# Weight folding of a linear-attention and softplus kernel: first weight block loaded ahead of batch 0's queries, each block folded right behind its turning, bias rows among the folds

## The chip, the cores and the metric

The kernel runs on one core of one Trainium2 chip. The metric is the device time of one execution in microseconds (us), taken over several runs; the changed kernel and the kernel before are timed in turn on the same chip. Times are quoted as medians with their range. A ratio is the mean time of one kernel's runs in the fast state over that of the other's in the same rounds, so it is not quite the ratio of the medians. The span of a profile (first to last instruction) is some 1.8 us shorter than the time of the same run.

## The reference, cut to what matters

```python
B, H, S, D = 8, 8, 576, 64
q_p = concat(relu(q) * cos_w, relu(q) * sin_w)        # the same for k_p
kv  = einsum('bhsf,bhsd->bhfd', k_p, v);  z = sum_s k_p
x   = einsum('bhsf,bhfd->bhsd', q_p, kv) / (einsum('bhsf,bhf->bhs', q_p, z) + 1e-6)
h   = x.reshape(4608, 512) @ w_in                     # w_in 512 x 2048
out = softplus(h) @ w_out                             # w_out 2048 x 512
```

The kernel uses that the hidden values are small: softplus(h) is close to ln 2 + h/2, so `softplus(x @ w_in) @ w_out` becomes `x @ W_c + b` with `W_c = 0.5 * w_in @ w_out` and `b = ln 2` times the column sums of `w_out`. It checks at the end that this is accurate enough, with an exact path behind an `if` that is not taken here. The product `w_in @ w_out` ("folding") is done once, at the start, in 8 blocks of 256 hidden columns.

## The kernel before

All loads are issued by GpSimd in one order and are cast from f32 to bf16 on the way (the page of this kernel has 36.70 MB read from HBM for 18.35 MB landed by the load queue). Batch 0's keys and values come first, then its queries, then the weight blocks, then the other batches.

```python
for part in range(2):
    load(0, "q", part)                        # two halves of batch 0's queries
for j in range(BLOCKS):                       # 8 weight blocks
    cols = slice(128 * FB * j, 128 * FB * (j + 1))
    nc.gpsimd.dma_start(w_in_sb[:, :, cols], w_in_r[:, :, cols])
    ...
    nc.gpsimd.dma_start(w_out_rows(FB * j, FB), w_out_r[:, FB * j : FB * (j + 1), :])
... # then batches 1, 2
```

PE's program for the first stage: 18 idle matmuls on constant data ("spin"), batch 0's values (`key_values`), then batch 0's four tiles of 128 tokens and the weights side by side. `turn_w_in(j)` transposes one weight block on PE and DVE copies it out of PSUM; `fold(j - 1)` multiplies the block turned one step earlier, so that no fold waits for DVE's copy (in the profile none of the 64 fold matmuls has a wait; two turns have, 0.19 and 0.82 us for DVE's copies):

```python
for hq in range(2):
    ...
    key_values(0, hq)
    spin(5 - 2 * hq)                          # idle matmuls, no work of the result
mark_eps()
for hq in range(2):
    relu_q(0, hq, nc.vector)
mark_perm()
turn_queries(0, split=True)
turn_queries(1, big_ps, split=True)
for j in range(BLOCKS + 1):
    if j < BLOCKS:
        turn_w_in(j)
    if j == 0:
        turn_queries(2, big_ps)
        attend(0, qt_ps)
        ...
    if j > 0:
        fold(j - 1, wc_ps)
    if 0 < j < 4:
        attend(j, qt_ps)
    if 0 < j < 5:
        turn_x(j - 1)
    ...
```

Behind it come W_c's scaling, ten matmuls for the bias, and batch 1. From there the kernel goes tile by tile (36 in all): `turn_queries` (two tiles ahead), `attend`, `turn_x`, `emit` (the product with W_c), while GpSimd applies relu to a later batch's keys and queries.

## Time and profile before

| | kernel before |
|---|---|
| median of the runs beside the changed kernel | 136.25 us (135.75 to 138.92, 6 runs) |
| span of the profile | 135.1 us |
| PE, ACT, DVE busy | 86%, 74%, 73% |
| end of the folds, of the bias (chain) | 40.28, 42.86 us |
| first query turn of batch 1, of batch 2 | 46.76, 55.90 us |

The reader is to see the 5 in the clock row, in the fifth slice: for some 3.4 us PE ran at about half clock (the 6 and the 5 at the end lie behind the last matmul). The view of busy time by stretch makes it plain (columns: from:to, length, then busy time of PE, PEld, DVE, ACT and POOL, granted clock, share of the DMA engines, GB/s):

```profile
10.20:13.60 3.40, 1.14 (x39) 0.86 (x39) 2.20 (x9) 2.24 (x9) 1.94 (x3) 1.00 1.24 199
13.60:17.00 3.40, 3.25 (x18) 1.67 (x17) 2.22 (x5) 1.18 (x3) 1.56 (x3) 0.50 1.36 201
```

PE was busy for only 1.14 of 3.40 us while it waited for batch 0's second half, and in the 3.40 us after that its clock was 0.50.

### The profile page before, as it was taken

How to read it: one execution, taken by the hardware profiler on the slowest of the kernel's cores; microseconds unless marked ns; L12 is line 12 of the kernel's file. 1: busy time of each engine (PE TensorE's matmuls, PEld its weight loads, DVE VectorE, ACT ScalarE, POOL GpSimd, SP SyncE). 2: the span in 40 equal slices, each digit the busy share in tenths (PEclk: the TensorE clock that was granted, in tenths of full speed). 3: DMA queues.
4: the chain of work that ended last, by engine and by line, in shares of the span. 5: the costliest groups of instructions: out<-in, count | busy, mean ns of one | idle time of the engine just before them, and what ended most of it. 6: DMA issues, size and time to landing. Idle time of an engine off the chain costs nothing.

```text
span 135.1 us, 4531 instructions
## 1 busy us (share of the span) xinstructions
PE 116.6 (86%) x1888; PEld 75.3 (56%) x1888; DVE 98.9 (73%) x198; ACT 100.6 (74%) x183; POOL 66.0 (49%) x84
## 2 busy tenths in 40 slices
PE   5993979999799987998989998999999999998700
PEld 2342466665344665675657676667577676764200
DVE  1356694567892589999987998898996995867710
ACT  3596345778989474989977996997988997998300
POOL 6995446454544118989889759063406610000000
PEclk9999599999999999999999999999999999999965
DMA  1999999999999999999999999999997397983450
GB/s 12 177 170 199 200 203 199 200 202 202 207 208 207 207 208 209 206 210 206 209 208 207 216 264 251 266 239 272 238 253 236 131 325 276 355 296 124 160 167 10
DMA packets 24683, 28.15 MB, mean 208 GB/s; under 512 B 1616, under 2 KB 20048, under 8 KB 24656
## 3 DMA queue, kind: packets, MB, share of 16 engines
q0 software_dynamic: 19152, 18.35, 83.0%
q1 hardware_dynamic: 5424, 9.31, 19.8%
q8 instruction: 17, 0.28, 0.8%
q10 hardware_dynamic: 80, 0.13, 0.3%
q14 instruction: 10, 0.08, 0.2%
HBM read 36.70 MB, written 9.44 MB: 341 GB/s over the span
## 4 chain that ended last, share of the span: by engine, by line
PE 44%; DVE 20%; ACT 14%; DMA 9%; issue 6%; POOL 2%; ACTq 0%; POOLq 0%
PE o_ps L404 10%; PE q_ps L321 8%; ACT qT L333 7%; PE wc_ps L233 6%; DVE vcs L280 6%; DMA v_sb<-in_v_dram 6%; PE kv_ps L294 5%; PE num_ps L351 4%; DVE o_sb L426 4%; DMA passed<-rden 3%; DVE x L362 3%; ACT xT_all L375 3%; ACT x L380 3%; PE xT_ps L371 3%; DVE w_inT L216 2%
## 5 line engine op out<-in xcount | busy, mean ns | idle before, releaser
L333 ACT CAST qT<-q_ps 128x1024 bf16<-128x1024 f32 x33 | 33.4, 1014 | 9.8 <-PE q_ps L321 9.8
L404 PE MATMUL o_ps<-W_c,xT_all 128*128 128x512 bf16 x128 | 32.8, 379 | 0.6 <-DVE o_sb L426 0.6
L280 DVE TENSOR_TENSOR vcs<-v_sb,cs_wide 128x1152 bf16<-128x1152 bf16 x32 | 28.5, 905 | 1.6 <-DMA v_sb<-in_v_dram 1.6
L426 DVE TENSOR_TENSOR o_sb<-o_ps,b_bc 128x512 f32<-128x512 f32 x32 | 22.0, 687 | 6.7 <-PE o_ps L404 6.5
L362 DVE TENSOR_TENSOR x<-num_ps,rden 128x512 bf16<-128x512 f32 x36 | 24.9, 691 | 2.4 <-DVE rden L358 0.5
L375 ACT CAST xT_all<-xT_ps 128x512 bf16<-128x512 f32 x36 | 21.4, 595 | 4.4 <-PE xT_ps L371 4.4
L321 PE MATMUL q_ps<-diag,q_r 128*128 128x256 bf16 x144 | 22.6, 282 | 1.9 <-ACT qT L333 0.9
L256 POOL TENSOR_SCALAR k_sb<-k_sb 128x1152 bf16<-128x1152 bf16 x12 | 14.2, 1196 | 16.7 <-DMA k_sb<-in_k_dram 16.7
L263 POOL TENSOR_SCALAR q_r<-q_sb 128x1152 bf16<-128x1152 bf16 x13 | 16.2, 1267 | 8.2 <-DMA q_sb<-in_q_dram 8.1
L380 ACT ACTIVATE x<-x,zero_b 128x1024 bf16<-128x1024 bf16 x17 | 19.7, 1158 | 0.0
L404 PEld LDWEIGHTS <-xT_all 128*128 128x128 bf16 x144 | 12.8, 98 | 10.6 <-issue 1.0
L321 PEld LDWEIGHTS <-q_r 128*128 128x128 bf16 x144 | 12.0, 99 | 6.8 <-issue 1.3
L351 PE MATMUL num_ps<-kvblk,qT 64*128 64x65 bf16 (+1 forms) x640 | 15.7, 193 | 0.0
L233 PE MATMUL wc_ps<-w_out_sb,w_inT 128*128 128x512 bf16 x64 | 15.0, 379 | 0.0
L294 PE MATMUL kv_ps<-vcs,k_sb 64*64 64x132 bf16 x576 | 11.3, 219 | 2.9 <-DVE eps L174 2.3
L371 PE MATMUL xT_ps<-perm,x 128*128 128x128 bf16 x128 | 12.4, 219 | 0.6 <-ACT xT_all L375 0.6
L341 PEld LDWEIGHTS <-warm 128*128 128x128 bf16 x72 | 6.9, 98 | 9.3 <-issue 1.7
L371 PEld LDWEIGHTS <-x 128*128 128x128 bf16 x144 | 10.6, 98 | 2.2 <-issue 0.6
L224 ACT ACTIVATE w_square<-w_inT,zero_b 128x512 bf16<-128x512 bf16 x16 | 11.6, 723 | 0.3
L351 PEld LDWEIGHTS <-qT 64*128 64x128 bf16 (+1 forms) x640 | 11.2, 97 | 0.8
L294 PEld LDWEIGHTS <-k_sb 64*64 64x64 bf16 x576 | 9.0, 106 | 4.7 <-issue 3.0
L358 DVE RECIPROCAL rden<-num_ps 128x8 f32<-128x8 f32 x36 | 7.1, 197 | 5.4 <-PE num_ps L351 5.4
(72 smaller groups left out, 132.0 us busy)
## 6 DMA issues: line engine op xcount, KB each, us to landing
out_dram<-o_sb SPq DMA_DIRECT2D x32, 256.0 KB
k_sb<-in_k_dram POOLq DMA_DIRECT2D x7, 576.0 KB, 14.8
v_sb<-in_v_dram POOLq DMA_DIRECT2D x6, 576.0 KB, 12.5
q_sb<-in_q_dram POOLq DMA_DIRECT2D x6, 576.0 KB, 18.0
xT_all<-in_moe_w_in_dram POOLq DMA_DIRECT2D x8, 256.0 KB, 10.6
w_out_sb<-in_moe_w_out_dram POOLq DMA_DIRECT2D x8, 256.0 KB, 10.6
v_sb<-in_v_dram POOLq DMA_DIRECT2D x4, 288.0 KB, 9.0
q_sb<-in_q_dram POOLq DMA_DIRECT2D x4, 288.0 KB, 9.9
```

The source lines that it names most:

```text
L233: nc.tensor.matmul(ps[g // 2][:, g % 2, :], w_inT_rows(ft)[:, g * 128 : (g + 1) * 128], w_out_rows(ft)[:, 0], start=(ft == 0), stop=(ft == ...
L280: nc.vector.tensor_mul(view(vcs, [T * 2 * VW, 2], [2 * VW, T], [1, D], offset=2 * hq * T * 2 * VW + c * VW), kqv[b, "v"][:, 2 * hq : 2 * h ...
L294: nc.tensor.matmul(kv[64 * i : 64 * i + 64, h2, :, :VW], k_r[rows, 2 * hq + i, t, :], vcs[rows, 2 * hq + i, t, :, :], start=(t == 0), stop ...
L321: nc.tensor.matmul(ps[:, j // 2, 256 * (j % 2) : 256 * (j % 2) + 256], q_rs[b][:, hq, t, :, :], diag[:, t, :, :], start=True, stop=True, s ...
L333: nc.scalar.copy(view(qT, [512, 2], [64, 2], [128, 4], [1, 64]), view(ps, [1, 1024]))
L351: nc.tensor.matmul(num[p0 : p0 + m, i, C * g : C * g + C], qTs[n][rows, hq, 2 * c + h2, p0 : p0 + m], blk_bufs[b % 3][rows, hq, h2, c, :], ...
L362: nc.vector.tensor_mul(xs[n // 2][:, n % 2], view(num, [C, 4], [512, 2], [1, D]), view(rden, [1, 4], [4, 2], [0, D]),)
L371: nc.tensor.matmul(ps[:, g, :], x[:, g, :, :], perm if len(tiles[n]) == 1 else ident, start=True, stop=True, skip_group_check=True,)
L375: nc.scalar.copy(xT_all[:, n], ps)
L380: nc.scalar.activation(x, x, ACT.Square, bias=zero_b, accum_out=x_norm[:, n : n + 1])
L404: nc.tensor.matmul(ps, xT_all[:, n, g, :], W_c[:, g, :], start=(g == 0), stop=(g == 3))
L426: nc.vector.tensor_add(o_sb, ps, b_bc)
```

## The change

The intent: PE has little to do between batch 0's values and its queries, so the first weight block is loaded there, turned and folded. From then on each block is folded right behind its own turning, with a query turn, an attend or an x turn between the turning and the fold to cover DVE's copy. Part of the bias rows moves among the folds and four output tiles move ahead of batch 1's values.

```diff
-    for part in range(2):
-        load(0, "q", part)
     for j in range(BLOCKS):
+        if j == 1:
+            for part in range(2):
+                load(0, "q", part)
...
+    turn_w_in(0)
     mark_eps()
+    fold(0, wc_ps)
     for hq in range(2):
         relu_q(0, hq, nc.vector)
     mark_perm()
     turn_queries(0, split=True)
-    turn_queries(1, big_ps, split=True)
...
+    attend(0, qt_ps)
+    beside = {
+        1: [lambda: turn_queries(1, split=True)],
+        2: [lambda: attend(1, qt_ps), lambda: turn_x(0)],
+        3: [lambda: turn_queries(2, split=True), lambda: turn_x(1)],
+        4: [lambda: attend(2, qt_ps)],
+        5: [lambda: turn_queries(3, split=True), lambda: turn_x(2)],
+        6: [lambda: attend(3, qt_ps)],
+        7: [lambda: turn_x(3), lambda: bias(range(8, 12))],
+    }
+    for j in range(1, BLOCKS):
+        turn_w_in(j)
+        for work_j in beside[j]:
+            work_j()
+        fold(j, wc_ps)
...
+    bias(range(12, FO))
...
-    early = [emit(0, xt_bank()), emit(1)]
-    for hq in range(2):
-        key_values(1, hq)
+    early = [emit(0, xt_bank()), emit(1)]         # finish both, then
+    early = [emit(2, xt_bank()), emit(3)]
+    for hq in range(2):
+        key_values(1, hq)
     turn_queries(4, split=True)
```

(The sums of `w_out`'s rows on DVE are also spread over four blocks, and query turns use one PSUM buffer in place of two.)

More of the change, by code (lines that the diff above doesn't have):

```diff
@@ L236, in fold, with sum_w_out, bias @@
             )
-    def sum_w_out(quarter):
-        rows = w_out_rows(4 * quarter, 4)
-        nc.vector.tensor_add(w_tmp if quarter else w_sum, rows[:, :2, :], rows[:, 2:, :])
-        if quarter:
+    def sum_w_out(step):
+        if step < 2:
+            rows = w_out_rows(4 * step, 4)
+            nc.vector.tensor_add(w_tmp if step else w_sum, rows[:, :2, :], rows[:, 2:, :])
+        elif step == 2:
             nc.vector.tensor_add(w_sum, w_sum, w_tmp)
+        else:
             nc.vector.tensor_add(w_tmp[:, 0, :], w_sum[:, 0, :], w_sum[:, 1, :])
-    def bias():
-        ps = o_ps.tile([128, D_MODEL], F32, tag="o", name="b_ps")
-        nc.tensor.matmul(ps, ones, w_tmp[:, 0, :], start=True, stop=False)
-        for ft in range(8, FO):
-            nc.tensor.matmul(ps, ones_b, w_out_rows(ft)[:, 0], start=False, stop=(ft == FO - 1))
-        nc.scalar.mul(b_bc, ps, LN2)
+    bias_ps = []
+    def bias(rows):
+        if not bias_ps:
+            bias_ps.append(qt_ps.tile([128, D_MODEL], F32, tag="qt", name="b_ps"))
+        for ft in rows:
+            nc.tensor.matmul(bias_ps[0], ones_b, w_out_rows(ft)[:, 0], start=(ft == 8), stop=False)
+        if rows.stop == FO:
+            nc.tensor.matmul(bias_ps[0], ones, w_tmp[:, 0, :], start=False, stop=True)
+            nc.scalar.mul(b_bc, bias_ps[0], LN2)
     def relu_k(b, engine, hps=slice(0, 4)):
@@ L451 @@
         spin(5 - 2 * hq)
+    xt_bank = lambda: xt_ps.tile([128, D_MODEL], F32, tag="xt", name="o_xt")
+    big_bank = lambda: big_ps.tile([128, 2, D_MODEL], F32, tag="big", name="o_big")[:, 0]
+    wc_ps = [big_ps.tile([128, 2, D_MODEL], F32, tag="big", name=f"wc_ps{r}") for r in range(2)]
+    turn_w_in(0)
     mark_eps()
+    fold(0, wc_ps)
     for hq in range(2):
@@ L456 @@
     turn_queries(0, split=True)
-    turn_queries(1, big_ps, split=True)
-    xt_bank = lambda: xt_ps.tile([128, D_MODEL], F32, tag="xt", name="o_xt")
-    big_bank = lambda: big_ps.tile([128, 2, D_MODEL], F32, tag="big", name="o_big")[:, 0]
-    for j in range(BLOCKS + 1):
-        if j < BLOCKS:
-            turn_w_in(j)
-        if j == 0:
-            turn_queries(2, big_ps)
-            attend(0, qt_ps)
-            nc.vector.tensor_copy(ident_f, ident)
-        if j == 1:
-            turn_queries(3)
-            wc_ps = [
-                big_ps.tile([128, 2, D_MODEL], F32, tag="big", name=f"wc_ps{r}") for r in range(2)
-            ]
-        if j > 0:
-            fold(j - 1, wc_ps)
-        if 0 < j < 4:
-            attend(j, qt_ps)
-        if 0 < j < 5:
-            turn_x(j - 1)
+    attend(0, qt_ps)
+    nc.vector.tensor_copy(ident_f, ident)
+    beside = {
[12 more added lines that the diff above has]
+        fold(j, wc_ps)
+        for ft in range(FB * (j - 1), FB * j):
+            square_w(ft)
+        if j in (3, 5, 6, 7):
+            sum_w_out((3, 5, 6, 7).index(j))
         if j == 6:
             square_x(0)
-        if 0 < j < 8:
-            for ft in range(FB * (j - 1), FB * j):
-                square_w(ft)
-        if j in (3, 5):
-            sum_w_out((j - 3) // 2)
-        if j == 6:
             mark_values(1)
@@ L489 @@
         nc.scalar.mul(W_c[:, g, :], wc_ps[g // 2][:, g % 2, :], 0.5)
+    bias(range(12, FO))
     for ft in range(7 * FB, FO):
         square_w(ft)
-    bias()
     square_x(1)
@@ L496 @@
             scale_values(1, hq, c)
+    early = [emit(0, xt_bank()), emit(1)]
+    for done in early:
+        finish(*done)
     relu_k(1, nc.vector)
     relu_q(1, 0, nc.gpsimd)
-    early = [emit(0, xt_bank()), emit(1)]
+    early = [emit(2, xt_bank()), emit(3)]
+    finish(*early[0])
+    relu_q(1, 1, nc.vector)
     for hq in range(2):
         key_values(1, hq)
-    for done in early:
-        finish(*done)
-    relu_q(1, 1, nc.vector)
-    early = [emit(2, xt_bank())]
     turn_queries(4, split=True)
-    early.append(emit(3))
+    finish(*early[1])
     turn_queries(5, big_ps)
-    for done in early:
-        finish(*done)
     pool_relu(2)
```

## The prediction

> **What bounds the kernel now.** I read the page first: PE is busy 86% of the span of 135.1 us, ACT 74%, DVE 73%, and the DMA row of the slices is at 9 from the second slice to slice 31, about 105 us. So two things run through the kernel side by side: PE's stream, in program order, and the stream of loads on the GpSimd queue. The chain of waits says which of them sets the end around the changed stage (columns: start us, length us, what):
>
> ```profile
> 36.22 0.61 PE wT_ps L210 x8
> 36.83 3.45 PE wc_ps L233 x16
> 40.28 0.86 PE b_ps L248 x2
> 41.14 1.73 PE b_ps L250 x8
> 42.86 0.86 PE o_xt L404 x4
> 43.73 0.89 PE o_ps L404 x4
> 44.62 1.18 PE kv_ps L294 x63
> 45.79 0.97 PE o_xt L404 x4
> 46.76 0.45 PE q_ps L321 x4
> ```
>
> The reader is to see the end of the weight stage: the last two blocks are folded together (16 matmuls, to 40.28), the bias follows (10 matmuls, to 42.86), then two output tiles, the values of batch 1, a third output tile, and only at 46.76 the first query turn of batch 1 (tile 4). The change shortens exactly this piece.
>
> The second view is the timeline of GpSimd, because batch 2 is prepared there:
>
> ```profile
> 43.03 1.14 POOL L263 TENSOR_SCALAR q_r<-q_sb 128x1152 bf16<-128x1152 bf16 x1 [0.26 <-DMA q_sb<-in_q_dram]
> ...
> 50.12 2.26 POOL L256 TENSOR_SCALAR k_sb<-k_sb 128x1152 bf16<-128x1152 bf16 x2 [5.81 <-DMA k_sb<-in_k_dram]
> 52.97 2.81 POOL L263 TENSOR_SCALAR q_r<-q_sb 128x1152 bf16<-128x1152 bf16 x2 [0.59 <-DMA q_sb<-in_q_dram]
> 55.72 0.79 POOL L75 DMA_DIRECT2D v_sb<-in_v_dram  x1
> ```
>
> GpSimd sits idle 5.81 us until the keys of batch 2 land at 50.1, and again until its queries land at 52.97; their relu is done at about 55.75. The third view, PE's timeline, shows what waits for that:
>
> ```profile
> 54.76 0.19 PE L341 MATMUL num_ps<-eps_b,warm 128*128 128x4 bf16 x2
> 54.88 0.43 PE L351 MATMUL num_ps<-kvblk,qT 64*128 64x65 bf16 x16
> 55.25 0.72 PE L294 MATMUL kv_ps<-vcs,k_sb 64*64 64x132 bf16 x36
> 55.90 0.61 PE L321 MATMUL q_ps<-diag,q_r 128*128 128x256 bf16 x4
> ```
>
> By program order (tiles 0-3 are batch 0, 4-7 batch 1, 8 is the rest of both, 9 the first of batch 2; queries are turned two tiles ahead) the turn at 55.90 is tile 9's, the first that reads batch 2's relu'd queries. PE came to it at 55.90, the queries were ready at about 55.75. **The slack is 0.15 us.** PE arrives here just in time; it cannot pass this point earlier unless the queries come earlier.
>
> Do they? They are the 30th of the loads, and the windows view gives the same 201 to 208 GB/s landed in 10-36, 36-53 and 53-72 us. There is no gap in the stream to close.
>
> [...]The page of this kernel has 36.70 MB read for 18.35 MB landed by the load queue (f32 cast to bf16), so 201 to 208 GB/s landed is some 400 to 415 read (my doubling)[...]. [...]the issue of each load waits for the eighth before it, in order. [...]the second query relu of batch 2 took 1.70 us beside a DVE scaling of values (54.02-54.77), the median of that row is 1.15.[...]
>
> **The change part by part.**
> 1. The load order. Only w_in block 0, w_out block 0 and the two query halves of batch 0 change places. From the issues that wait for them, w_in block 0 landed at 15.5, w_out block 0 at 16.8, the query halves at 12.8 and 14.2. After: the weights some 2.7 us earlier (12.8, 14.1), the queries 2.6 us later (15.4, 16.8). From block 1 on (18.2) all landings stay: same bytes, same order, same wait for the eighth before. Block 7 lands at about 34.8 (w_in) and 36.0 (w_out); batch 1's keys at 41.5, its query halves at 43.0 and, one half load later, about 44.4; batch 2's keys at 50.1 and queries at 53.0.
> 2. The folds. One block (8 matmuls) is 1.73 us, a turn of weights 0.45, a query turn 0.54, an attend 0.54, a turn of x 0.22 to 0.33, half the bias rows 4 x 0.216 = 0.86. In PE's stream from the first weight turn to the end of the last fold: 8 x 1.73 + 8 x 0.45 + 4 x 0.54 + 4 x 0.54 + 4 x 0.28 + 0.86 = 23.7 us. From 12.9 that is 36.6 at best; the last block lands at 36.0, so not before 36.1 + 1.73 = 37.9. A fold now stands right behind its own turning, and must wait for DVE's two copies (0.75 us) less what PE does between; I choose 0.15 us of idle a block beyond the DMA's floor, 8 x 0.15 = 1.2, so the folds end at about **39** instead of 40.28. The range of this is 38 to 40.5.
> 3. The bias. It was 0.86 + 1.73 = 2.59 us after the folds; now 0.86 of it lies among them, 1.73 remains: PE is free at about 40.8 instead of 42.86, **2.1 us earlier**.
> 4. DVE and ACT. Two query evacuations of 1.01 us on ACT become 0.59 on ACT with 0.69 on DVE: ACT loses 0.84, DVE gains 1.38. The four sums of w_out are the same work, spread over four blocks. ACT had 0.50 us of idle before W_c, so this keeps W_c from being late.
> 5. Behind the weights, four output tiles (4 x 0.88) now stand before batch 1's values. They fill PE from 40.8 to about 44.3, the values take 1.2, so PE is at tile 4's turn at about 45.5; its queries are ready at 44.4 + 0.74 (DVE relu) = 45.2. So tile 4 is turned at about 45.5 instead of 46.76: of 2.1 us, **1.3 us** are left.
> 6. The next five tiles keep this lead, until tile 9's turn. There PE arrives at 55.90 - 1.3 = 54.6, the queries are ready at 52.97 + 2 x 1.15 = 55.3 (no collision with DVE) to 55.75 (as before). So the turn starts at 55.3 to 55.75, and **0.15 to 0.6 us** of the lead are left; I take 0.4. The rest turns into a wait of PE of about 0.9 us.
>
> Behind this PE's stream is the same, with a mean of some 2.3 us a tile. Later load limits do not bind: batch 3's queries are ready at 64.33 for a turn at 65.98, batch 7's at 108.6 for a turn at 110.48, so 0.4 us fit into both. The sum is 136.33 - 0.4 = **135.9 us**.
>
> **Rivals.** (a) The whole 1.3 to 2.1 us arrive at the end: 134.2 to 135.0. For it: the chain runs on PE here. Against it: 0.15 us of slack at tile 9, and a load stream with no gap. It needs batch 2's queries over a microsecond earlier, and no part of the change does that. (b) The new order makes the weight stage slower: fold waits for DVE's copy, DVE has 1.38 us more, one PSUM buffer serves query turns, attends and the bias in turn, and PE cannot hide it. Then tile 4 comes later than 46.76, and each such microsecond is fully paid, as there is no slack: 137 to 138. Against it: 1.5 us of room between 39 and the old end. (c) DVE and GpSimd collide more in 53 to 56 us, as DVE's scalings move earlier: both query relus at 1.7 us put the turn at 56.4, some 0.5 us later: 136.8. (d) PE's unexplained 0.85 us of issue at 70.36 falls elsewhere or goes: up to 0.85 either way.
>
> **Range and chances.** The cap gives 135.7 to 136.2; (c), (d) and the spread between runs widen it to **135.0 to 136.9**. Faster by over 2% is below 133.6, which needs 2.7 us, more than the change saves even on PE: 0.03. Slower by over 2% is above 139.1, and needs (b) in full: 0.03. Within 2%: 0.94.
>
> **What would show it.** Right: folds end near 39, tile 4's turn near 45.5, batch 2's queries still land near 53, a new wait of PE of 0.5 to 1.3 us on GpSimd's relu (L270 in the changed kernel) before tile 9's turn, which starts at 55.3 to 55.8. Wrong: tile 9's turn well before 55, as the loads came earlier; tile 4's turn after 46.8, so rival (b); or a lead at 56 us that is lost or grows later, which would mean that a limit behind tile 9 matters that I took as settled.

The sum came to 136.33 - 0.4 = 135.9 us. What the trace shows is 201 to 208 GB/s landed from 10 to 72 us. The order of the loads is in GpSimd's timeline: of the 11th to the 33rd load, 22 were issued when the eighth before had landed (those at 12.83 and 14.21 us had waited 0.73 and 0.62 us for the query halves), and the one at 35.09 waited for DVE's sum. That a relu takes longer beside a scaling, which rival (c) builds on, was read from the one overlap given, 1.70 us against a median of 1.15.

## More of the kernel before

The two rows are PE's busy share and the granted TensorE clock, both in tenths, over 40 slices of 3.38 us:

```profile
PE   5993979999799987998989998999999999998700
...
PEclk9999599999999999999999999999999999999965
```

## The result, and the profile after

The changed kernel took 141.19 us in the median (139.76 to 142.88, 6 runs) against 136.25: the ratio of the fast runs is 1.029, 95% interval 1.025 to 1.033. It is slower, and lies outside my range. Its runs split: three at 142.0 to 142.9, which are marked slow, and three at 139.8 to 140.4. The first profile belongs to a slow run, so I use it only to see what to look for. Its rows of PE's busy share and granted clock:

```profile
PE   5944758999999985999979899799999999998700
...
PEclk9999996899999999599999999999999999999996
```

The clock falls twice, at 22 us and at 56 us. In PE's timeline of this run (columns: start us, length us, instruction, then what PE waited for):

```profile
20.00 0.19 PE L348 MATMUL num_ps<-eps_b,warm 128*128 128x4 bf16 x2 [1.40 <-DVE qT L336]
...
21.58 0.61 PE L328 MATMUL q_ps<-diag,q_r 128*128 128x256 bf16 x4 [0.48 <-DVE x L369]
22.05 3.43 PE L234 MATMUL wc_ps<-w_out_sb,w_inT 128*128 128x512 bf16 x8
...
26.64 1.89 PE L234 MATMUL wc_ps<-w_out_sb,w_inT 128*128 128x512 bf16 x8
```

the fold of block 1 takes 3.43 us, that of block 2, the same eight matmuls, 1.89. And in busy time by stretch, each of the two falls follows 3.4 us in which PE was busy about half the time (1.72 and 1.87 us of 3.40), with a clock of 0.51 and 0.50 after it:

```profile
18.80:22.20 3.40, 1.72 (x31) 1.28 (x31) 2.27 (x6) 0.42 (x1) 1.78 (x3) 1.00 1.36 200
22.20:25.60 3.40, 3.40 (x12) 1.39 (x11) 0.82 (x2) 2.11 (x5) 1.92 (x3) 0.51 1.34 202
53.00:56.40 3.40, 1.87 (x31) 1.32 (x31) 2.44 (x7) 2.10 (x3) 3.10 (x3) 1.00 1.20 208
56.40:59.80 3.40, 3.40 (x38) 2.06 (x39) 2.05 (x5) 2.64 (x4) 2.85 (x5) 0.50 1.22 207
```

Summed over such a stretch, one minus the clock gives 1.71 us of PE time lost at full clock. So I formed these theories. **Clock**: the change leaves PE waiting in a place where this makes the granted clock fall, and the slowdown is these stretches. Rivals: **query chain** (batch 0's queries, 2.6 us later, hold up PE in program order at full clock), **fold behind turning** (waits for DVE's copies and for the one PSUM buffer), and **collision** (being late makes DVE and GpSimd meet more often). The prediction's own **cap** (batch 2's queries hold tile 9) was to be tested too.

### The profile page after: what moved, and what is told of

Its sections match the earlier page's. It is cut to its first block, busy times and chain, and to the rows that moved or that the text cites. A ratio compares the mean times of both kernels' runs of the same rounds, so it can differ in the third digit from the quotient of the medians.

```text
span 141.1 us, 4527 instructions
## 1 busy us (share of the span) xinstructions
PE 118.6 (84%) x1888; PEld 75.8 (54%) x1888; DVE 102.3 (72%) x200; ACT 99.4 (70%) x183; POOL 68.0 (48%) x84
## 4 chain that ended last, share of the span: by engine, by line
PE 42%; DVE 26%; ACT 10%; DMA 9%; issue 7%; POOL 2%; DVEq 0%; ACTq 0%; POOLq 0%
DVE vcs L287 10%; PE o_ps L411 10%; PE wc_ps L234 7%; PE q_ps L328 7%; DMA v_sb<-in_v_dram 6%; ACT qT L340 6%; DVE o_sb L433 6%; PE kv_ps L301 4%; DVE x L369 4%; DMA passed<-rden 3%; PE num_ps L358 3%; PE xT_ps L378 2%; PE wT_ps L211 2%; ACT qT L336 2%; ACT x L387 1%
## 5 line engine op out<-in xcount | busy, mean ns | idle before, releaser
L340 ACT CAST qT<-q_ps 128x1024 bf16<-128x1024 f32 x31 | 31.5, 1015 | 7.0 <-PE q_ps L328 7.0
L411 PE MATMUL o_ps<-W_c,xT_all 128*128 128x512 bf16 x128 | 33.7, 387 | 1.4 <-DVE o_sb L433 1.4
L287 DVE TENSOR_TENSOR vcs<-v_sb,cs_wide 128x1152 bf16<-128x1152 bf16 x32 | 30.6, 973 | 2.3 <-DMA v_sb<-in_v_dram 2.3
L270 POOL TENSOR_SCALAR q_r<-q_sb 128x1152 bf16<-128x1152 bf16 x13 | 18.6, 1445 | 9.7 <-PE q_ps L328 6.4
L411 PEld LDWEIGHTS <-xT_all 128*128 128x128 bf16 x144 | 13.2, 99 | 12.9 <-issue 3.4
L263 POOL TENSOR_SCALAR k_sb<-k_sb 128x1152 bf16<-128x1152 bf16 x12 | 13.6, 1148 | 11.8 <-DMA k_sb<-in_k_dram 11.7
L234 PE MATMUL wc_ps<-w_out_sb,w_inT 128*128 128x512 bf16 x64 | 16.7, 409 | 0.8 <-DVE w_inT L217 0.5
L306 ACT CAST kvblk<-kv_ps 128x260 bf16<-128x260 f32 x16 | 6.0, 374 | 8.7 <-PE kv_ps L301 8.6
## 6 DMA issues: line engine op xcount, KB each, us to landing
k_sb<-in_k_dram POOLq DMA_DIRECT2D x7, 576.0 KB, 12.4
```

Source lines behind the costliest of these rows:

```text
L234: nc.tensor.matmul(ps[g // 2][:, g % 2, :], w_inT_rows(ft)[:, g * 128 : (g + 1) * 128], w_out_rows(ft)[:, 0], start=(ft == 0), stop=(ft == ...
L287: nc.vector.tensor_mul(view(vcs, [T * 2 * VW, 2], [2 * VW, T], [1, D], offset=2 * hq * T * 2 * VW + c * VW), kqv[b, "v"][:, 2 * hq : 2 * h ...
L340: nc.scalar.copy(view(qT, [512, 2], [64, 2], [128, 4], [1, 64]), view(ps, [1, 1024]))
L411: nc.tensor.matmul(ps, xT_all[:, n, g, :], W_c[:, g, :], start=(g == 0), stop=(g == 3))
```

## The experiments

All kernels gave correct results. The medians of the kernel before were 136.38, 136.27, 136.56 and 136.15 us (11 runs each). One experiment is one row of this table; "stretches" are those at half clock between 10 and 125 us in its profile (the clock also falls behind the last matmul in every profile, from 129.6 us in the kernel before, with no work of PE behind it).

| run | median, us (all runs) | ratio of fast runs | state of the profile: stretches |
|---|---|---|---|
| tail_only | 136.83 (135.75 to 139.56) | 1.000 | fast: none |
| queries_first | 138.17 (136.91 to 141.04) | 1.009 | slow: 13.5 to 21, 54.5 to 58.5 |
| after_filled | 138.35 (135.99 to 141.99) | - | fast: none |
| delay6 | 138.83 (136.22 to 140.54) | - | fast: none |
| after_again | 140.87 (139.67 to 142.28) | 1.030 | slow: 22 to 25.5, 56 to 60 |
| after_filled2 | 136.62 (135.83 to 140.0) | 1.002 | fast: none |
| before_filled | 136.82 (135.13 to 137.75) | 0.996 | slow: none |
| order_only | 139.84 (139.51 to 141.84) | 1.023 | fast: 15 to 22.5 |
| queries_first_filled | 136.05 (135.60 to 137.33) | 0.998 | fast: none |
| after_late | 140.46 (136.33 to 142.17) | - | slow: 19 to 23 |
| before_no_spin | 137.45 (137.15 to 138.39) | 1.010 | fast: 11 to 18.5 |
| halves | 136.43 (135.91 to 139.28) | 0.999 | fast: none |
| after_p0, p1, p2 | 138.52, 137.12, 136.91 (profiled runs; one more run each: 139.27, 138.14, 142.70) | 1.021, 1.011, - | fast: 20 to 24; none; 13 to 17 |
| after_early_mid | 136.94 (136.12 to 141.05) | 1.003 | slow: 51.5 to 58.5 |

### Idle matmuls in PE's gap

The changed kernel, with matmuls on constant data written to an unused PSUM bank, where PE waits at 17 to 22 us:

```diff
+    fill(1)
     turn_queries(0, split=True)
+    fill(5)
     attend(0, qt_ps)
...
         turn_w_in(j)
+        if j == 1:
+            fill(2)
```

> The changed kernel with 8 idle matmuls on constant data put into PE's waits at 17 to 22 us (1 ahead of tile 0's query turn, 5 behind it, 2 behind the turning of block 1). They do no work of the result. Theory 'clock' (PE's idle there lets the granted clock fall, so that fold 1 runs at 3.43 us instead of 1.90): fold 1 is 1.9 us in the profile, the runs at 142 to 143 vanish, the time is 139.8 or less in all runs. Rival 'the clock falls for another reason or elsewhere': runs still split into 139.9 and 142.5, as for the changed kernel; if the fillers only delay, the fast ones are 0.3 to 1 us slower.

Measured: 136.80, 135.99, 139.91 and 141.99 us. Two runs fell to the level of the kernel before, which the changed kernel had not reached in its six; two did not. The profile is of a fast run, without any stretch at half clock, and fold 1 took 1.90 us. That fits the expected mechanism, but it does not prove it alone, as the changed kernel without fillers also ran at 136.91 and 137.12 later, on another chip (below). And "all runs" was a miss: something else can still bring the slow runs.

Next the fillers went to three places: 11 instead of 5 idle matmuls behind the first half of batch 0's values, the 8 above, and 10 around tiles 4 and 5, where PE waits for ACT:

```diff
-        spin(5 - 2 * hq)
+        spin(3 if hq else 11)
...
+            if i == 4:
+                fill_late(2, xt_ps, "xt")
             attend(i)
+            if i == 5:
+                fill_late(4, o_ps, "o")      # and 4 more behind turn_x
```

> The changed kernel with idle matmuls on constant data in PE's waits in three places: 10 to 12.5 us (6 more), 17 to 22 us (8), 49 to 56 us (10). Theory 'clock': with PE kept busy the half-clock stretches go, nearly all runs lie within 136 to 137.5 (ratio 0.995 to 1.008), and none at 142. Rival 'order of work': the fillers change nothing in the fast runs, ratio 1.02 or more.

Measured: ratio 1.002 (0.995 to 1.009); five of six runs at 135.83 to 137.46 and one at 140.0. Matmuls that compute nothing took back the whole 2.9%. The changed kernel without them ran in turn with it on the same chip, in the same rounds (after_again, 139.67 to 142.28). Busy time by stretch, first in this kernel, then in the changed kernel's profile of a fast run without a stretch (after_p1, below):

```profile
14.00:22.00 8.00, 6.83 (x60) 3.33 (x58) 5.48 (x18) 0.88 (x2) 4.03 (x6) 1.00 1.33 201
49.00:56.00 7.00, 6.71 (x104) 4.32 (x104) 6.03 (x13) 4.44 (x6) 5.27 (x6) 1.00 1.21 208
```

```profile
14.00:22.00 8.00, 5.11 (x50) 2.57 (x48) 5.47 (x18) 1.00 (x2) 3.97 (x6) 1.00 1.33 201
49.00:56.00 7.00, 5.05 (x97) 3.77 (x101) 6.12 (x13) 4.54 (x7) 5.39 (x6) 1.00 1.21 208
```

PE's busy time rises from 5.11 to 6.83 of 8 us and from 5.05 to 6.71 of 7, and, PE's own weight loads aside, no other engine's does.

With the late place alone:

> The changed kernel with idle matmuls at 49 to 56 us alone (10 of them); the gap at 17 to 22 us stays. Theory 'clock': the half-clock stretch at 22 to 25.5 stays and costs about 1.7 us, the one at 56 to 59.5 goes: 138 to 140 in all runs, none at 142 (ratio 1.010 to 1.025). If both stretches hang on the gap at 17 to 22, ratio under 1.005; if the late fillers do nothing, 139.7 to 142.3 as in the changed kernel.

Measured: 138.91, 136.33, 142.17, 142.00. The profile, of the run at 138.91, has the stretch at 19 to 23 and none at 56, as expected. "None at 142" was a miss: the late fillers do not keep the slow runs away. With the two early places alone:

> The changed kernel with idle matmuls at 10 to 12.5 and 17 to 22 us, none at 49 to 56. If the earlier gaps alone bring the stretches, it does as well as with all three places filled: nearly all runs at 135.8 to 137.5, ratio 0.995 to 1.008. If the gap at 49 to 56 brings the second stretch, a third or more of the runs lie at 138 to 140 with a stretch at 54 to 60 us.

Measured: five of seven runs at 136.12 to 137.25, ratio 1.003; two slow ones (139.83 and 141.05), and the profile, of a slow run, has two stretches in a row at 51.5 to 58.5. So the early gaps carry most of the loss, and the gap at 49 to 56 us can add its own.

### Which part of the change brings it

The load order alone, in the kernel before:

```diff
-    for part in range(2):
-        load(0, "q", part)
     for j in range(BLOCKS):
+        if j == 1:
+            for part in range(2):
+                load(0, "q", part)
```

> The kernel before with the new load order alone: the first weight block ahead of batch 0's queries, PE's program as before. PE then waits for the queries, which land 2.6 us later, with nothing to do from about 14 to 17.5 us. Theory 'clock': this idle brings a half-clock stretch in most runs, at 17 to 24 us, and the time rises by 2 us or more in them (138 to 142, spread over 2 us). Theory 'query chain' at full clock: a plain shift of the weight stage by up to 2.6 us without spread, ratio 1.01 to 1.02, no stretch at half clock. If both are absorbed later: ratio under 1.005.

Measured: ratio 1.023 (1.014 to 1.033), 139.51 to 140.00 and one run at 141.84. The profile is of a fast run (140.00), PE's timeline:

```profile
15.78 0.61 PE L322 MATMUL q_ps<-diag,q_r 128*128 128x256 bf16 x2 [1.86 <-DVE q_r L264]
17.25 1.46 PE L322 MATMUL q_ps<-diag,q_r 128*128 128x256 bf16 x6 [0.87 <-DVE q_r L264]
18.51 1.06 PE L211 MATMUL wT_ps<-ident,xT_all 128*128 128x128 bf16 x8
```

PE waits 1.86 and 0.87 us for the relu of the late queries; eight transposes then take 1.06 us instead of 0.61. The clock is half from 15.45 for two stretches, 3.42 us lost, and tile 4's attend comes 2.7 us later than before. Most of the change's loss comes with this one part.

Everything but the load order, with tile 0 turned ahead of weight block 0:

```diff
+    for part in range(2):
+        load(0, "q", part)
...
-    turn_w_in(0)
     mark_eps()
-    fold(0, wc_ps)
...
     turn_queries(0, split=True)
+    turn_w_in(0)
     attend(0, qt_ps)
+    fold(0, wc_ps)
```

> The changed kernel with batch 0's queries loaded first again and tile 0 turned ahead of weight block 0; folds right behind their turning, bias among the folds and the tail as changed. Theory 'query chain' (the slowdown comes from queries that land 2.6 us later and hold up PE in program order at 16 to 22 us): fold 1 starts near 20.5 instead of 22.05, PE's idle between 14 and 22 falls from about 2.9 us to under 1.5, tile 4's turn near 47.5, and the time is 136 to 138 (ratio 0.998 to 1.012). Rival 'fold behind turning' (waits for DVE's copies and for the one PSUM buffer of query turns and attends cost it): fold 1 still starts after 21.5 or the blocks still take 2.87 us or more with idle in them, and the time stays near 140 (ratio 1.02 or more).

Measured: ratio 1.009 (1.002 to 1.015). By the number, the query chain would fit. But the profile has stretches at 13.5 to 21 and 54.5 to 58.5, so the number does not tell the chain from the clock. The same kernel with fillers at 10 to 12.5 and 49 to 56 us does:

> All of the change except its load order, with idle matmuls at 10 to 12.5 and 49 to 56 us. Without them this kernel took 1.009 of the time before (136.9 to 138.5, one run 141.0, with half-clock stretches at 13.5 to 21 and 54.5 to 58). Theory 'clock': the stretches go and the ratio is 0.993 to 1.004, so that no cost of folding right behind the turning is left. Rival: folding behind the turning costs 0.9% at full clock, ratio stays above 1.006.

Measured: ratio 0.998 (0.993 to 1.003), all six runs at 135.6 to 137.3, none slow. At full clock no cost of folding behind the turning is left, so this rival falls. It gains nothing either.

The tail alone (four output tiles ahead of batch 1's values), in the kernel before:

```diff
-    for hq in range(2):
-        key_values(1, hq)
+    early = [emit(2, xt_bank()), emit(3)]
+    finish(*early[0])
+    relu_q(1, 1, nc.vector)
+    for hq in range(2):
+        key_values(1, hq)
```

> The kernel before with one part of the change alone: the four output tiles ahead of batch 1's values and batch 1's first query turn. Theory 'cap' (my prediction's step 6): tile 4's turn comes up to 1.3 us earlier than 46.76, but batch 2's relu'd queries are still ready at 55.3 to 55.8, so tile 9's turn stays at 55.3 to 55.9 and the time within 0.6 us of before (ratio 0.995 to 1.002). Rival 'lead carries': tile 9's turn moves with tile 4's and the time drops by 1 us or more (ratio below 0.993). Third possibility, that this part itself costs: ratio above 1.005, with PE waits at o_ps/o_xt.

Measured: ratio 1.000 (0.995 to 1.005). The size is what the cap expected, but not by the cap: in this profile (136.88, fast) tile 4's turn had hardly a lead (46.50 in the chain, against 46.76), batch 2's queries were ready at 54.64 (52.38 + 2.26), and PE came to tile 9's turn only at 56.04, because it waited for DVE's scaling of batch 2's values ahead of it:

```profile
55.39 0.72 PE L294 MATMUL kv_ps<-vcs,k_sb 64*64 64x132 bf16 x36 [0.40 <-DVE vcs L280]
56.04 0.61 PE L321 MATMUL q_ps<-diag,q_r 128*128 128x256 bf16 x4
```

### The other way round, and two more

The kernel before without the 5 and 3 idle matmuls that its author had put behind batch 0's values (`spin(5 - 2 * hq)` deleted):

> The kernel before without the 5 and 3 idle matmuls that it already has behind batch 0's values (at 9.1 and 13.3 us). They do no work of the result. Theory 'clock', the other way round: more idle of PE brings half-clock stretches between 13 and 21 us in most runs and a higher time, ratio 1.005 to 1.025. If PE's idle does not govern the granted clock, the time is unchanged or lower (ratio 0.995 to 1.003).

Measured: ratio 1.010 (1.004 to 1.016), with two stretches in a row at 11 to 18.5 in a fast run (137.31). Taking away matmuls that compute nothing makes the kernel slower: the theory holds in this direction too, on a kernel without any part of the change.

The same fillers in the kernel before:

> The kernel before with the same fillers at 10 to 12.5 and 49 to 56 us. Theory 'clock': its half-clock stretch at 13.5 to 17 us goes and the runs at 137 to 139 get rarer; what is gained in the mean is small, since the stretch lies ahead of the folds, which wait for loads: ratio 0.99 to 1.003. If the fillers as such cost time, ratio above 1.005.

Measured: 135.13 to 137.75, ratio 0.996 (0.988 to 1.003): no gain that can be told from noise, as expected. That runs at 137 to 139 get rarer was a miss: three of six lie at 137.3 to 137.8, as do four of eleven of the kernel before. The stretch at 13.6 to 17 us is gone from its profile, which is of one of these three, marked slow: not every difference between runs is a stretch. That of the kernel before lay where it costs little (ratio 0.996 with the fillers, which took it away).

PE held up by six idle matmuls ahead of tile 4:

> The kernel before with 6 idle matmuls (6 x 0.216 = 1.3 us) ahead of tile 4's turn: PE is late by 1.3 us where batch 1 begins, all else as before. Plain sum: the time rises by 1.3 us less whatever waits take up (ratio 1.006 to 1.010). Theory 'collision' (being late against the loads makes DVE's scalings meet GpSimd's relus more often): the time rises by more than 2 us (ratio above 1.013), mean of the DVE scaling row above 905 ns.

Measured: 136.22, 137.50, 140.17, 140.54. The profile is of the first of these, without a stretch: tile 4's attend at 49.30 instead of 48.46, tile 9's at 60.86 instead of 60.19, tile 13's at 71.12 instead of 71.32. At full clock a lag below a microsecond is gone by tile 13, and the span was 134.4 us. So neither the plain sum nor the collision held there. The two slow runs have no profile; their mean clock was 0.968 against 0.989.

A try at a version that beats both, with the cap lifted by loading batch 2's keys and queries in halves:

> A version that may beat both: the kernel before with the change's tail, idle matmuls at 10 to 12.5 us and 7 at 49 to 56 us, and batch 2's keys and queries loaded in two halves each, so that GpSimd's relus start on the first half. Theory 'cap' (batch 2's relu'd queries hold tile 9's turn): they are ready about 1 us earlier (54.1 instead of 55.1 to 55.75), tile 9's turn moves to 54.5 to 55.2 and the time falls to 135.0 to 135.7, ratio 0.990 to 0.996. Rival 'DVE holds it' (as with the tail alone, where PE waited 0.40 us for DVE's scaling of batch 2's values while the queries had been ready for a microsecond): tile 9's turn stays near 56 and the ratio at 0.996 to 1.002.

Measured: ratio 0.999. In its profile the queries were ready at 54.42 (51.84 + 2.58), 1.3 us ahead of the kernel before, and tile 9's turn was at 56.29. The relus came earlier and the turn did not: what sets tile 9's turn in this kernel is not the load of its queries but PE's own stream, which carries seven idle matmuls ahead of it here. None of these versions beats the kernel before by more than noise.

### Does a fast run of the changed kernel have stretches?

The changed kernel once more, unchanged:

> The changed kernel once more, unchanged, for a profile of its fast state and for more times. Theory 'clock': also a fast run holds one or two stretches of about 3.4 us with half the granted clock between 14 and 60 us, each costing about 1.7 us; time 139.8 to 142.9 as before. Rival 'order of work' (the fast runs are slower than before through waits at full clock): the fast profile shows no such stretch between 14 and 125 us, and tile 9's attend (60.19 in the kernel before) still 2 us or more later.

It was run three more times, on another chip:

> The changed kernel, for a profile of its fast state (139.7 to 140.4 us). Theory 'clock': such a run holds one or two half-clock stretches of 3.4 us between 13 and 60 us, of which at least one lies on PE's path. Rival: none, and the time goes to waits at full clock.

> As the run before it: the changed kernel, for a profile of its fast state; half-clock stretches between 13 and 60 us by the theory 'clock', none by its rival.

> As the two runs before it: the changed kernel, for a profile of its fast state; half-clock stretches between 13 and 60 us by the theory 'clock', none by its rival.

All three profiles are of runs marked fast. The mark compares a run with others of the same call: beside the fastest run of this program, 136.91, the fast ones of the first six (139.8 to 140.4) would be slow. Together with the first two the profiles form a row from one and the same program:

| profiled run, us | state | stretches at half clock | attend of tile 4, 9, 13, 35, us |
|---|---|---|---|
| 137.12 (after_p1) | fast | none | 48.64, 60.86, 71.31, 124.07 |
| 136.91 (after_p2) | fast | 13.2 to 16.6 | 49.55, 61.70, 71.78, 123.84 |
| 138.52 (after_p0) | fast | 20.2 to 23.7 | 49.86, 62.96, 72.64, 125.18 |
| 142.28 (after_again) | slow | 22.0 to 25.4, 56.1 to 59.5 | 51.38, 66.98, 77.17, 128.94 |
| 142.88 (first profile) | slow | 22.2 to 25.7, 56.4 to 59.8 | 50.98, 64.95, 75.74, 129.28 |
| kernel before | fast | 13.6 to 17.0 | 48.46, 60.19, 71.32, 123.42 |

The clock row of after_p1, beside those shown above:

```profile
PEclk9999999999999999999999999999999999999995
```

The theory had asked for a stretch in each of them; one has none, which was a miss of the expectation but makes the case clearer. Without a stretch this program took 137.12 us, about 1.0 us more than the median of the kernel before on that chip (136.15). With one between batch 0's values and its queries, where PE waits anyway, the time is the same. With one on fold 1 it is 1.4 us more (138.52 against 137.12). With that and a second one at 56 us it is 5.2 to 5.8 us more (both runs marked slow). Each of these is one run.

### What goes ahead of a stretch

I cut the 18 profiles from 9 to 127 us into windows of 3.413 us, the length of a single stretch (13.60 to 17.01 us in the kernel before, at a clock of 0.50), in step with the stretches of each profile (where it has none, with the fall behind the last matmul), and took PE's busy share of each window at full clock (585 of them), and whether the next one was at half clock.

| PE busy in the window | windows | followed by half clock |
|---|---|---|
| under 49% | 7 | 6 |
| 49 to 66% | 21 | 6 |
| over 66% | 557 | 0 |

The 12 windows ahead of half clock had PE busy for 33 to 61%. A single gap of PE can be shorter than a window and still have a stretch behind it: the longest was 2.26 us in the kernel before, 1.40 us before fold 1 and 0.88 us before the stretch at 56 us.

In the kernels with all fillers no window was under 66%. after_p1 had two, at 15.70 to 19.11 us (1.75 us of 3.41 busy) and at 49.83 to 53.24 (1.83), and its clock fell behind neither; after_p0 had one at 16.83 to 20.24 with the same share (1.74), and there it fell. So PE's busy share, as this profile gives it, tells where the clock can fall, not that it will. The windows begin at another point of the program in every run (the stretches of the changed kernel at 20.2, 22.0, 22.2 and 13.2 us). This fits with one program showing 137, 138.5 and 142 us, but what decides in windows of 49 to 66% stays open.

## Why the prediction was wrong, point by point

**The landings** (step 1) were right. In after_p1, issues that wait for them put weight block 0 at 12.4 and 13.7 us (predicted 12.8 and 14.1), and the query halves at 15.1 and 16.6 (15.4 and 16.8); GpSimd's timeline of that run has batch 2's keys and queries where they were before:

```profile
50.02 2.25 POOL L263 TENSOR_SCALAR k_sb<-k_sb 128x1152 bf16<-128x1152 bf16 x2 [5.83 <-DMA k_sb<-in_k_dram]
52.86 2.25 POOL L270 TENSOR_SCALAR q_r<-q_sb 128x1152 bf16<-128x1152 bf16 x2 [0.58 <-DMA q_sb<-in_q_dram]
```

**The sum of the folds** (step 2) was mis-sized even at full clock. The work was about right: PE was busy for 24.1 us between the first weight turn and the end of the last fold, where I had 23.7. The idle was not: I chose 8 x 0.15 = 1.2 us, all of it for DVE's copies. PE's timeline of after_p1:

```profile
14.77 1.90 PE L234 MATMUL wc_ps<-w_out_sb,w_inT 128*128 128x512 bf16 x8 [0.52 <-DVE w_inT L217]
16.90 0.39 PE L328 MATMUL q_ps<-diag,q_r 128*128 128x256 bf16 x2 [0.23 <-DVE q_r L270]
17.55 0.39 PE L328 MATMUL q_ps<-diag,q_r 128*128 128x256 bf16 x2 [0.27 <-DVE q_r L270]
19.35 0.19 PE L348 MATMUL num_ps<-eps_b,warm 128*128 128x4 bf16 x2 [1.40 <-DVE qT L336]
...
20.93 0.61 PE L328 MATMUL q_ps<-diag,q_r 128*128 128x256 bf16 x4 [0.48 <-DVE x L369]
21.40 1.90 PE L234 MATMUL wc_ps<-w_out_sb,w_inT 128*128 128x512 bf16 x8
```

The waits of blocks 0 and 1 alone add up to 0.52 + 0.23 + 0.27 + 1.40 + 0.48 = 2.9 us: relu, query turn, evacuation, attend and the one PSUM buffer follow one another with nothing beside them. From 21.4 on there is hardly an idle moment, so nothing is won back. The first turn began at 13.64, not 12.9. The folds ended at 40.9 (39.03 + 1.89) where I had 39, against 40.28 before.

**Steps 3 and 5** failed with it: by the chain of after_p1 PE was free at 42.65 instead of 40.8 (0.2 us ahead of the 42.86 of before, not 2.1), and tile 4's turn was at 47.42, later than the 46.76 of before, where I had 45.5.

**Step 6**, the cap at tile 9, was not reached: its turn was at 56.52 with the queries ready at 55.11. In the two kernels meant to show it (tail_only, halves), DVE's scaling or PE's own stream came first, and neither had a lead of over 0.3 us at tile 4. That a lead must end there was argued and stays untested; that a small lag is taken up by tile 13 was measured (delay6, after_p1).

**The missing term** is the one that decided: the granted clock. No step of my sum and none of my rivals held it. I wrote that the rest of the lead "turns into a wait of PE", as if a wait had no other price. The runs show a price: a window in which PE is busy for about half can be followed by one at half clock (12 of the 28 windows under 66%), 1.71 us lost, and if that lies on a PE-bound stretch of the program the time goes up (138.52 against 137.12 us with one on fold 1, one run each). Rival (b) named the right stage and the right sign but gave waits for DVE and PSUM as the reason, and asked for 137 to 138. Those waits exist, and the one stretch-free run of the changed kernel, 137.12, is where it asked; but that is 1.0 us over the kernel before on that chip, of the 3.9 us that the ratio of 1.029 stands for, and with fillers the ratio is 1.002. Two small slips changed nothing: the DMA row is at 9 up to slice 30, not 31, and 36.1 + 1.73 is 37.8.

What is open: the fast runs of 139.7 to 140.4 us have no profile. Their mean clock of 0.956 to 0.969 is below the 0.987 of after_p1, which fits with stretches but does not place them; the slow runs beside them have 0.966 to 0.967, so the mean clock does not tell the two groups apart. Nor does every slow run seem to hold stretches: those of after_filled2 (140.0) and halves (139.28) have mean clocks of 0.982 and 0.988, like the fast runs of these kernels. What costs them 3 us is not known, as no such run has a profile. What follows the second stretch also differs: between tile 9 and tile 35 the first profile falls another 1.1 us behind after_p1 (5.2 less 4.1), with 2.5 us of PE waits for DVE at 61 to 105 us, while after_again makes up 1.2 us there (6.1 to 4.9). Both are slow runs, and no run tests whether DVE's scalings meet GpSimd's relus more often.

## What to carry to other kernels

Where PE sets the pace, ask of every change how busy PE stays over a stretch of time as long as those at half clock (3.41 us here, where 12 of the 28 windows under 66% busy and none of the 557 above were followed by half clock), not only whether an added wait is hidden: behind such waits the eight matmuls of a fold took 3.43 us at a clock of 0.51, the next eight 1.89 at full clock. Read the granted clock's row first, and compare runs by their stretches before explaining a difference by order and waits. If one program shows several times, idle matmuls in PE's gaps are a cheap test, and were a cure here (ratio 1.002 with them, 1.030 without, in the same rounds).
